# Talking-heads attention before a feed-forward block: values' products of a pair of heads in two halves over two turns

## The chip, the cores and the metric

One core of one Trainium2 chip runs the whole program. The metric is the device time of one execution in microseconds (us), taken over several runs; the profile is of one further execution. The engines are TensorE (PE; its weight loads are shown as PEld), VectorE (DVE), ScalarE (ACT), GpSimd (POOL) and SyncE (SP), whose queue issues most of the DMAs.

## The reference

Four batches, 12 heads, 448 tokens, 64 values a head. The heads are mixed twice: the scores before the softmax (w_pre) and the weights after it (w_post).

```python
scores = scale * np.matmul(q, k.transpose(0, 1, 3, 2))
scores = np.einsum('bhij,hg->bgij', scores, w_pre)
scores = scores - np.max(scores, axis=-1, keepdims=True)
attn = np.exp(scores)
attn = attn / (np.sum(attn, axis=-1, keepdims=True) + 1e-09)
attn = np.einsum('bhij,hg->bgij', attn, w_post)
out = np.matmul(attn, v)             # then (tokens, 768) = x
g = x @ w_gate
silu = g * (1.0 / (1.0 + np.exp(-g)))
y = silu * (x @ w_val) @ w_out
```

## The kernel before, in words

The attention works in **turns**. A turn belongs to one **unit** of 20 tokens of one batch (two tiles of 10 tokens); there are 23 units in a batch, the last of 8 tokens. Each engine runs its instructions in the order in which they are issued, and that order is written out by hand: `at(key, fn)` puts a step at a key, the steps are sorted by key, and a turn is two keys long (`slot(u)` is the key at which the turn of unit u begins; batch b begins at key 45 b, so the short turn 22 is only one key ahead of turn 0 of the next batch). Unit and turn numbers below start with 0 in each batch.

What one turn holds, in the order of its keys:

- `gather` of the unit three turns ahead: 448 KB of scores, which lie in DRAM as rows (token, head), come to SBUF as `rs` (L305). It goes through SP's queue.
- `pre` (key + 0.5, L324): the head mixing w_pre, as 4 products on PE, into two PSUM banks of the tag "pre".
- `qk` (+ 0.55, L275): scores of a group of rows for a unit many turns ahead, into two banks "qk"; VectorE or ScalarE copy them to `stg` (L284, L286), and `store` writes 448 KB to DRAM. Turns 14 to 22 do this for the next batch, turns 0 to 11 for their own; turns 12 and 13 have no scores to make.
- `kprep` (+ 0.65, L228): in turns 10 to 15, the transposes of the keys of one pair of heads of the next batch; `qprep` (+ 0.66, L245): in eight turns of a batch, the transposes of half a block of queries. Both write a bank of the tag "tr", which VectorE empties (`kcopy`, L236, and `qcopy`, L252).
- `top` and `expo` (+ 0.6 and + 0.95): VectorE's row maximum (L335) and ScalarE's exponential (L341) of the two `pre` banks; `norm`: the reciprocal on VectorE and `rw`, w_post divided by the sums, on POOL (L352).
- `post` (L368): 28 small products that mix the exponentials of a unit by `rw`, into the two banks "post"; ScalarE copies them to `attnT` (`mixed`, L383). Its key is that of its own unit + 5.2, which is two turns later, + 1.2: behind `pre`, `qk` and the transposes of that turn.
- `av` (+ 1.3, L410): the products of the mixed weights with the values of one pair of heads, 16 products (32 records) over 240 or 208 tokens, into two banks of the tag "tr" (one for each tile of a unit, r = 0 and 1). Twelve turns of a batch have one: turns 14 to 19 for the first 240 tokens, turns 2 to 7 of the next batch for the rest. `values` (+ 1.9) copies the banks out on ScalarE (L445; L454 and VectorE's L456 for batches 2 and 3).

`attnT` holds 18 units as a ring of three segments; where an `av` wraps round its end, the copies out are in more pieces. The eight PSUM banks are qk 2, pre 2, post 2, tr 2. Batch 3 does its `av` in another pattern at its end, which the change leaves as it is. The feed-forward part follows, and its weights are converted beside the last batch.

Of the kernel before, what the change touches and what calls it, by code (L numbers as in the profile page):

```python
# [24 lines left out]
def talking_heads_moe_kernel(ctx, tc, q, k, v, w_pre, w_post, w_gate, w_val, w_out, out):  # L25
# [25 lines left out]
    NSEG = 3  # L51
# [36 lines left out]
    rsp = pool(right, "rsp", 6, "right")  # L88
    ep = pool(right, "ep", 6, "right")
# [17 lines left out]
    attnT = cst.tile([P, NSEG * SU, NSL, TS], F32, name="attnT")  # L107
    mixing = []

    def mixing_loads():  # L110
        for t, value in ((copies, 0.0), (blocks, 1.0), (wpre, 0.0), (wpost, 0.0)):
            nc.gpsimd.memset(t, value)
        for x, r in itertools.product(range(2), range(2)):
# [38 lines left out]
    qn, kn, vn, kk, qt, stg, rs, pts, sts, et, rw, ats, trs, qtrs, qks = ({} for _ in range(15))  # L152
# [11 lines left out]
    def load_v(b, c):  # L164
        full = S - PART
        if b not in vn:
            vn[b] = vp.tile([P, H, NC, D], F32, tag="vn", name=f"vn_{b}")
        if c < NC:
            hs = slice(c * (H // NC), (c + 1) * (H // NC))
            nc.sync.dma_start(  # L170
                out=vn[b][:, hs, :NC - 1].rearrange("p h c d -> p h (c d)"),
                in_=v[b, hs, :full].rearrange("h (p c) d -> p h (c d)", c=NC - 1),
            )
        else:
            r = c - NC
            nc.sync.dma_start(
                out=vn[b][r * HB:(r + 1) * HB, :, NC - 1], in_=v[b, :, full:].rearrange("h p d -> p h d")
            )
# [6 lines left out]
    def load_k(b, p, part=None, eng=nc.sync):  # L185
# [13 lines left out]
        else:  # L199
# [3 lines left out]
            t = nat.tile([P, n], F32, tag="kn", name=f"kn_{b}_{p}", bufs=6)  # L203
# [34 lines left out]
    def qprep(b, c, g):  # L238
# [3 lines left out]
        tr = ps.tile([P, NPAIR // 2, P], F32, tag="tr", name=f"qtr_{b}_{c}_{g}")  # L242
# [18 lines left out]
    def qk(b, c, g):  # L261
        o, pairs = groups(b, c)[g]
        bank = "qk"
        if b == 0 and c < 2 and (c + g) % 2:
            bank = "pre" if c else "tr"
        pt = [
            ps.tile([P, S], F32, tag=bank, name=f"qk_{b}_{c}_{g}_{x}")
            for x in range(2)
# [10 lines left out]
        stg[b, c, g] = nat.tile([P, 2, S], F32, tag="stg", name=f"stg_{b}_{c}_{g}", bufs=6)  # L279
# [65 lines left out]
    def norm(b, u):  # L345
# [4 lines left out]
        for r, t in enumerate(tiles_of(u)):  # L350
            w = rw[b, t] = smp.tile([P, H, HS], F32, tag="rw", name=f"rw_{b}_{t}", bufs=6)
# [24 lines left out]
    def mixed(b, u, y):  # L376
        pt = ats[b, u][y]
        seg, i = divmod(u, SU)
        i += (b * NC + seg) % NSEG * SU
        m = min(HS, rows(2 * u) - y * HS)  # L380
        full = len(tiles_of(u)) == 2
        for part, n0, n1 in ((P, 0, NSL),) if full else ((P, 0, (NC - 1) * H), (HB, (NC - 1) * H, NC * H)):
            nc.scalar.activation(attnT[:part, i, n0:n1, y * HS:y * HS + m], pt[:part, n0:n1, :m], AF.Copy)  # L383
# [4 lines left out]
    def av(b, c0, m, p):  # L388
        n = -(-cols(c0, m) // TS)
        w = SEG // (3 - m)  # L390
        pt = [ps.tile([P, S], F32, tag="tr", name=f"av_{b}_{c0}_{p}_{r}")[:, :SEG] for r in range(2)]
        first = (b * NC + c0) % NSEG
        wrapped = first + m > NSEG
        ring = attnT.rearrange("p (s u) z i -> p s u z i", s=NSEG)
        u0 = first * SU
        for c in range(NC):
            for x in range(3 - m):
                for r in range(2):
                    k = (n + 1 - r) // 2
                    part = slice(r * HB, (r + 1) * HB) if c == NC - 1 else slice(P)  # L400
                    for j in range(2):
                        h = 2 * (p + x) + j
                        js = slice(j * D, (j + 1) * D)
                        if wrapped:
                            o = pt[r][js].rearrange("p (s u i) -> p s u i", s=2, i=TS)
                            a = ring[part, 0:NSEG:NSEG - 1, :, place(r, c) + h]
                        else:
                            o = pt[r][js, x * SEG // 2:x * SEG // 2 + k * TS].rearrange("p (u i) -> p u i", i=TS)
                            a = attnT[part, u0:u0 + k, place(r, c) + h]
                        nc.tensor.matmul(o, vn[b][part, h, c], a, start=(c == 0 and x == 0), stop=(c == NC - 1 and x == 2 - m))  # L410
        avs[b, c0, p] = pt, c0, m, wrapped

    def spread(av, *to):
        pt, c0, m, wrapped = av
        n = cols(c0, m)
        full, rest = divmod(n, 2 * TS)
        for r in range(2):
            if wrapped:
                v = pt[r].rearrange("p (s u i) -> p s u i", s=2, i=HS)
                for s in range(2):  # L420
                    yield v[:, s], *(
                        d[:, 0].rearrange("p (s u r i) -> p s u r i", s=2, r=2, i=HS)[:, 1 - s, :, r] for d in to
                    )
            else:
                v = pt[r].rearrange("p (x u i) -> p x u i", x=3 - m, i=HS)
                yield v[:, :, :2 * full], *(
                    d[:, :, :2 * full * TS].rearrange("p x (u r i) -> p x u r i", r=2, i=HS)[:, :, :, r] for d in to
                )
        if rest and wrapped:
            v = pt[0].rearrange("p (s u i) -> p s u i", s=2, i=TS)[:, 0, full - SU, :rest]  # L430
            yield v, *(d[:, 0, n - rest:n] for d in to)
        elif rest:
# [651 lines left out]
```

## Time and profile before

| | us |
|---|---|
| median of three runs | 898.02 |
| lowest, highest run | 894.50, 1346.31 |
| the profiled execution's own time | 896.03 |
| its span, first to last instruction | 894.2 |
| PE busy in the span | 855.1 |

The profiled execution lasted 1.8 us longer than its span. The attention takes about the first 400 us of the span, the feed-forward block the rest. A stretch that is called a period below is from the start of `pre` in turn 14 of a batch to the same point of the next batch. Starts in the rows are us from the start of the span.

### The profile page before, as it was taken

The numbers are of one execution on the slowest core, as the hardware profiler recorded it, in microseconds if no ns is written. First come the engines' busy times: TensorE is split into PE (matmuls) and PEld (weight loads), VectorE is DVE, ScalarE is ACT, GpSimd is POOL, SyncE is SP. The second block draws the span as 40 slices with busy tenths as digits, with TensorE's granted clock in tenths as the row PEclk, the third lists the DMA queues.
The fourth block names the chain that finished last, engine by engine and source line by source line (L and its number), as shares of the span: only waits on it lengthen the run. The fifth ranks groups of instructions, "written<-read, shape, count | busy, mean of one in ns | idle before, by whom it ended". The sixth has DMA issues, their size and how long they took to land.

```text
span 894.2 us, 26476 instructions
## 1 busy us (share of the span) xinstructions
PE 855.1 (96%) x10886; PEld 703.9 (79%) x10886; DVE 643.5 (72%) x1159; ACT 458.8 (51%) x1042; POOL 175.9 (20%) x255
## 2 busy tenths in 40 slices
PE   8589999999999997989999999999999999999998
PEld 5255666566656665668999999999999999999998
DVE  3476575657666765567999999678999969775843
ACT  3375677667766767653343333254454455353321
POOL 2011111111111111114555453111101112002020
PEclk9698999999999999999999999999999999999999
DMA  9898998989897869344998886446755579988696
GB/s 213 290 297 266 297 283 282 330 265 296 277 336 234 272 211 315 133 146 151 302 313 252 253 285 174 155 154 209 226 183 179 184 271 324 320 281 194 185 285 157
DMA packets 186033, 218.72 MB, mean 245 GB/s; under 512 B 58136, under 2 KB 153400, under 8 KB 185912
## 3 DMA queue, kind: packets, MB, share of 16 engines
q1 hardware_dynamic: 178856, 205.91, 71.7%
q0 software_dynamic: 3168, 8.26, 5.4%
q10 hardware_dynamic: 3888, 2.86, 1.2%
q8 instruction: 86, 1.41, 0.6%
q14 instruction: 35, 0.29, 0.1%
HBM read 138.15 MB, written 77.47 MB: 241 GB/s over the span
## 4 chain that ended last, share of the span: by engine, by line
PE 80%; DMA 8%; DVE 5%; ACT 3%; issue 2%; SPq 0%; POOL 0%; DVEq 0%; ACTq 0%; POOLq 0%
PE pre L324 8%; PE av L410 8%; PE post L368 7%; PE qk L275 6%; PE p L711 6%; PE p L710 6%; PE p L713 6%; PE q L854 4%; PE q L853 4%; PE q L852 4%; PE upv L766 3%; PE upv L765 3%; PE upv L769 3%; PE upg L769 3%; PE upg L765 3%; PE upg L766 3%
## 5 line engine op out<-in xcount | busy, mean ns | idle before, releaser
L335 DVE TENSOR_REDUCE st<-pre 128x1 f32<-128x448 f32 x180 | 104.4, 620 | 78.0 <-PE pre L324 71.7
L341 ACT ACTIVATE e<-pre,st 128x448 f32<-128x448 f32 x180 | 112.7, 631 | 83.3 <-DVE st L335 75.2
L608 POOL TENSOR_SCALAR mag<-mag 128x768 f32<-128x768 f32 x33 | 99.8, 3024 | 257.0 <-ACT mag L606 227.4
L368 PEld LDWEIGHTS post<-rw,e 60*64 60x64 f32 x5040 | 98.7, 136 | 36.4 <-issue 26.7
L352 POOL TENSOR_SCALAR rw<-w_post_gs,st 128x60 f32<-128x60 f32 x180 | 55.6, 324 | 332.8 <-DVE st L349 270.9
L324 PE MATMUL pre<-rs,w_pre_blocks 64*64 64x448 f32 (+1 forms) x720 | 106.7, 569 | 13.4 <-DMA rs<-s_all 8.5
L368 PE MATMUL post<-rw,e 60*64 60x60 f32 x5040 | 105.7, 223 | 8.5 <-issue 4.5
L383 ACT ACTIVATE attnT<-post 128x420 f32<-128x420 f32 (+1 forms) x192 | 91.2, 542 | 23.0 <-PE post L368 22.5
L275 PE MATMUL qk<-kk,qt 64*64 64x448 f32 x672 | 94.4, 547 | 0.4 <-DVE w_post_gs L148 0.3
L854 PE MATMUL q<-ohi,al 128*128 128x384 f32 x276 | 93.3, 338 | 1.4 <-DVE al L837 1.4
L852 PE MATMUL q<-ohi,ah 128*128 128x384 f32 x276 | 93.0, 337 | 0.6 <-ACT ah L845 0.5
L853 PE MATMUL q<-olo,ah 128*128 128x384 f32 x276 | 92.8, 336 | 0.0
L410 PE MATMUL av<-attnT,vn 128*64 128x120 f32 (+9 forms) x1728 | 88.7, 262 | 3.9 <-issue 2.2
L410 PEld LDWEIGHTS av<-attnT,vn 128*64 128x64 f32 (+1 forms) x1728 | 70.0, 135 | 16.3 <-issue 7.9
L284 DVE COPY stg<-qk 128x448 f32<-128x448 f32 x120 | 71.1, 618 | 8.3 <-PE qk L275 5.0
L845 ACT ACTIVATE ah<-ar 128x768 fp32r<-128x768 f32 x46 | 38.6, 843 | 57.6 <-PE q L853 28.8
L275 PEld LDWEIGHTS qk<-kk,qt 64*64 64x64 f32 x672 | 32.1, 134 | 35.3 <-issue 24.0
L837 DVE TENSOR_TENSOR al<-ar,ah 128x768 fp32r<-128x768 f32 x46 | 43.7, 953 | 15.5 <-ACT ah L845 15.5
L854 PEld LDWEIGHTS q<-ohi,al 128*128 128x128 f32 x276 | 51.8, 188 | 2.7 <-DVE al L837 2.7
L606 ACT ACTIVATE mag<-raw 128x768 f32<-128x768 f32 x36 | 32.8, 911 | 40.8 <-DVE w L620 27.8
L766 PE MATMUL upv<-x,wlo 128*128 128x448 f32 x144 | 52.8, 367 | 0.0
L765 PE MATMUL upg<-x,whi 128*128 128x448 f32 x144 | 52.8, 367 | 0.0
(141 smaller groups left out, 1676.8 us busy)
## 6 DMA issues: line engine op xcount, KB each, us to landing
rs<-s_all SPq DMA_DIRECT2D x88, 448.0 KB, 5.2
s_all<-stg SPq DMA_DIRECT2D x60, 448.0 KB, 5.1
w_d<-w SPq DMA_DIRECT2D x36, 384.0 KB, 4.0
raw<-in_moe_w_gate_dram SPq DMA_DIRECT2D x12, 768.0 KB, 5.3
raw<-in_moe_w_val_dram SPq DMA_DIRECT2D x12, 768.0 KB, 6.6
raw<-in_moe_w_out_dram SPq DMA_DIRECT2D x12, 768.0 KB, 5.8
w<-w_d SPq DMA_DIRECT2D x24, 384.0 KB, 5.8
s_all<-stg SPq DMA_DIRECT2D x39, 224.0 KB, 5.0
```

The lines of the kernel that those rows point to most:

```text
L275: nc.tensor.matmul(pt[x][i * HB:(i + 1) * HB], qt[b, c][hs, p, r:r + HB], kk[b, p][hs], start=True, stop=True)
L324: nc.tensor.matmul(pt[r][x * HB:(x + 1) * HB], wpre[i], xs[i, x], start=True, stop=True)
L335: nc.vector.tensor_reduce(sts[b, u][:, 0, r:r + 1], pts[b, t], axis=AX.X, op=ALU.max, negate=True)
L341: nc.scalar.activation(e, pts.pop((b, t)), AF.Exp, bias=st[:, 0, r:r + 1], scale=1.0, accum_out=st[:, 1, r:r + 1])
L368: nc.tensor.matmul(ats[b, u][y][o * HB:(o + 1) * HB, to, :m], et[b, t][i, c * P + x * HB:c * P + (x + 1) * HB], rw[b, t][i, :, :m], start= ...
L410: nc.tensor.matmul(o, vn[b][part, h, c], a, start=(c == 0 and x == 0), stop=(c == NC - 1 and x == 2 - m))
L608: eng.tensor_scalar(mag, mag, f32_of(0x38000000), f32_of(0x47EFFFFF), op0=ALU.max, op1=ALU.min)
L765: nc.tensor.matmul(pt, hi[:, c], xh[:, c, ts], start=(c == 0), stop=False)
L766: nc.tensor.matmul(pt, lo[:, c], xh[:, c, ts], start=False, stop=False)
L852: nc.tensor.matmul(pt, ahi, bhi, start=f == 0, stop=False)
L853: nc.tensor.matmul(pt, ahi, blo, start=False, stop=False)
L854: nc.tensor.matmul(pt, alo, bhi, start=False, stop=f == NFH - 1)
```

## The change

The ring goes: `attnT` holds all 23 units of a batch (16.8 KB more in each partition), so an `av` never wraps. To pay for it, the buffers of `rs`, `e` and `rw` go from 6 to 4, those of `kn` and `stg` from 6 to 5. In batches 0 to 2 each `av` is cut in two halves in two turns: the half for r = 0 (its three full blocks of keys), then that for r = 1 with the last block of keys for both. The halves lie in turns 13 to 22, 0 and 1 (first 240 tokens) and 2 (both halves of the first pair) to 12 (the rest). The two "tr" banks become one "av" (r = 0) and one "tr" (r = 1, and all transposes). `post` moves one key forward, to the head of its turn, ahead of `pre`. The first block of queries of the next batch is transposed in turns 7 and 9 in place of 11 and 12, and loaded earlier. The values of a batch come in 9 DMAs in place of 6, in three steps at turns 6.5, 9.5 and 13.25 in place of turns 8 to 12.

```diff
-    rsp = pool(right, "rsp", 6, "right")
-    ep = pool(right, "ep", 6, "right")
+    rsp = pool(right, "rsp", 4, "right")
+    ep = pool(right, "ep", 4, "right")
...
-    attnT = cst.tile([P, NSEG * SU, NSL, TS], F32, name="attnT")
+    attnT = cst.tile([P, NUB, NSL, TS], F32, name="attnT")
...
-            t = nat.tile([P, n], F32, tag="kn", name=f"kn_{b}_{p}", bufs=6)
+            t = nat.tile([P, n], F32, tag="kn", name=f"kn_{b}_{p}", bufs=5)
...
-            tr = ps.tile([P, S], F32, tag="tr", bufs=2, name=f"ktr_{b}_{p}")
+            tr = ps.tile([P, S], F32, tag="tr", bufs=1, name=f"ktr_{b}_{p}")
...
-        tr = ps.tile([P, NPAIR // 2, P], F32, tag="tr", name=f"qtr_{b}_{c}_{g}")
+        tr = ps.tile([P, NPAIR // 2, P], F32, tag="tr" if b or g == 0 else "av", bufs=1, name=f"qtr_{b}_{c}_{g}")
...
-        stg[b, c, g] = nat.tile([P, 2, S], F32, tag="stg", name=f"stg_{b}_{c}_{g}", bufs=6)
+        stg[b, c, g] = nat.tile([P, 2, S], F32, tag="stg", name=f"stg_{b}_{c}_{g}", bufs=5)
...
-    def av(b, c0, m, p):
+    def av(b, c0, m, p, steps=(0, 1)):
         n = -(-cols(c0, m) // TS)
-        pt = [ps.tile([P, S], F32, tag="tr", name=f"av_{b}_{c0}_{p}_{r}")[:, :SEG] for r in range(2)]
...
+        for r in steps:
+            avs[b, c0, p, r] = ps.tile([P, S], F32, tag=("av", "tr")[r], bufs=1, name=f"av_{b}_{c0}_{p}_{r}")[:, :SEG]
+        u0 = c0 * SU
+        for c in range(NC if 1 in steps else NC - 1):
             for x in range(3 - m):
-                for r in range(2):
+                for r in steps if c < NC - 1 else range(2):
...
-        for i, c in enumerate((NC, NC + 1, *range(NC))):
-            at(n0 + 16.2 + 1.6 * i if b else (-34.3, -34.29, -30.35, -30.34, -29.35, -29.34)[i], later(load_v, b, c))
+        if b:
+            for g, n in enumerate((13.0, 19.0, 26.5)):
+                at(n0 + n, later(load_v, b, g))
+                for r in range(2):
+                    at(n0 + n + 0.7 + 0.7 * r, later(load_v_last, b, r, g))
...
-            ready = (slot(BACK - NUB - 3), slot(BACK - NUB - 2)) if c == 0 else (at_k[0] - 2, at_k[2])
+            ready = (slot(BACK - NUB - 7), slot(BACK - NUB - 5)) if c == 0 else (at_k[0] - 2, at_k[2])
...
-            n1 = n + (5.2 if b < B - 1 or u < NUB - 3 else 4.2 if u == NUB - 3 else 3.2)
+            n1 = n + (4.2 if u < NUB - 2 else 3.2)
...
+            if b < B - 1:
+                for p in range(NPAIR):
+                    for i in range(2):
+                        u = 13 + 2 * p + i if c0 == 0 else NUB + 2 if p == 0 else NUB + 1 + 2 * p + i
+                        n = slot(u) if u < NUB else n0 + NTB + 2 * (u - NUB)
+                        at(n + 1.3, later(av, b, c0, m, p, (i,)))
+                    at(n + 1.9, later(values, b, c0, m, p))
+                continue
```

## Rows read from the trace of the kernel before

**Rows 1.** The page, busy time of the span: engine, us, share, instructions.
```profile
PE 855.1 (96%) x10886; PEld 703.9 (79%) x10886; DVE 643.5 (72%) x1159; ACT 458.8 (51%) x1042; POOL 175.9 (20%) x255
```

**Rows 2.** Windows of two periods: stretch, length, busy by engine, clock, DMA share, GB/s.
```profile
82.68:171.30 88.62, 86.98 (x2053) 58.68 (x2045) 56.74 (x140) 63.05 (x193) 13.59 (x45) 1.00 0.91 286
259.62:349.00 89.38, 84.23 (x2019) 56.29 (x2019) 58.97 (x170) 60.51 (x189) 13.59 (x45) 1.00 0.82 262
```

**Rows 3.** Windows of the period between, by turns 14-15, 16-19, 20-1, 2-7, 8-13.
```profile
171.30:182.02 10.72, 10.34 (x216) 6.83 (x220) 5.45 (x13) 6.03 (x17) 1.81 (x6) 1.00 1.02 320
182.02:199.69 17.67, 17.67 (x431) 12.40 (x427) 9.34 (x23) 12.07 (x35) 2.44 (x8) 1.00 0.86 252
199.69:213.71 14.02, 13.48 (x339) 9.48 (x332) 10.68 (x25) 10.52 (x29) 2.12 (x7) 1.00 0.87 275
213.71:239.85 26.14, 26.14 (x631) 17.59 (x634) 15.40 (x39) 18.02 (x60) 3.78 (x13) 1.00 0.87 288
239.85:259.62 19.77, 18.73 (x449) 11.79 (x442) 15.12 (x37) 14.91 (x42) 3.46 (x13) 1.00 1.09 336
```

**Rows 4.** Timeline of PE, turn 18 of batch 1: start, length, line, operation [idle].
```profile
190.91 0.93 PE L324 MATMUL pre<-rs,w_pre_blocks 64*64 64x448 f32 x8
191.66 0.94 PE L275 MATMUL qk<-kk,qt 64*64 64x448 f32 x8
192.42 1.00 PE L368 MATMUL post<-rw,e 60*64 60x60 f32 x56
193.34 1.82 PE L410 MATMUL av<-attnT,vn 128*64 128x120 f32 x32
194.98 0.56 PE L324 MATMUL pre<-rs,w_pre_blocks 64*64 64x448 f32 x4
```

**Rows 5.** Timeline of PE, products over 208 tokens, turn 6 of batch 2.
```profile
234.50 1.64 PE L410 MATMUL av<-attnT,vn 128*64 128x110 f32 x32
235.96 0.92 PE L324 MATMUL pre<-rs,w_pre_blocks 60*64 60x448 f32 x8
```

**Rows 6.** Timeline, turn 15 of batch 1: key transposes, two score copies on VectorE.
```profile
176.75 0.93 PE L324 MATMUL pre<-rs,w_pre_blocks 64*64 64x448 f32 x8
...
179.05 1.04 PE L368 MATMUL post<-rw,e 60*64 60x60 f32 x56
...
179.92 0.61 DVE L236 COPY kk<-ktr 128x448 f32<-128x448 f32 x1
...
180.59 0.51 PEld L410 LDWEIGHTS av<-attnT,vn 128*64 128x64 f32 x10 [0.37 <-DVE kk L236]
```

**Rows 7.** Timeline, turn 16 of batch 1: query transposes, one score copy on VectorE.
```profile
182.02 0.94 PE L324 MATMUL pre<-rs,w_pre_blocks 64*64 64x448 f32 x8
...
184.12 1.16 PE L368 MATMUL post<-rw,e 60*64 60x60 f32 x56
...
184.66 0.55 DVE L252 COPY qt<-qtr 128x384 f32<-128x384 f32 x1
```

**Rows 8.** Timeline, turn 14 of batch 1: key transposes, one score copy on VectorE.
```profile
171.30 0.98 PE L324 MATMUL pre<-rs,w_pre_blocks 64*64 64x448 f32 x8 [0.95 <-ACT attnT L383]
...
173.45 0.61 DVE L284 COPY stg<-qk 128x448 f32<-128x448 f32 x1
...
173.65 0.34 PE L368 MATMUL post<-rw,e 60*64 60x60 f32 x7
...
173.98 0.61 DVE L236 COPY kk<-ktr 128x448 f32<-128x448 f32 x1
```

**Rows 9.** Timeline of SP's queue, turns 13 to 15 of batch 1.
```profile
168.82 3.47 SPq L170 DMA_DIRECT2D vn<-in_v_dram  x1
173.86 1.20 SPq L305 DMA_DIRECT2D rs<-s_all  x2
...
177.87 0.75 SPq L305 DMA_DIRECT2D rs<-s_all  x1
```

**Rows 10.** The page, DMA issues: tile, count, KB each, median us to landing.
```profile
rs<-s_all SPq DMA_DIRECT2D x88, 448.0 KB, 5.2
```

**Rows 11.** Timeline, turn 10 of batch 0: first key transposes.
```profile
67.95 0.90 PE L228 MATMUL ktr<-ident,kn 128*128 128x128 f32 x3 [3.48 <-DMA kn<-in_k_dram]
```

**Rows 12.** Timeline of ACT at the start: the last copy of scores before turn 0.
```profile
24.84 0.54 ACT L286 ACTIVATE stg<-qk 128x448 f32<-128x448 f32 x1 [2.00 <-DMA s_all<-stg]
```

More of the change, by code (lines that the diff above doesn't have):

```diff
@@ L112, in mixing_loads @@
             nc.gpsimd.memset(t, value)
+        nc.gpsimd.memset(attnT[:, NUB - 1, :, S % TS:], 0.0)
         for x, r in itertools.product(range(2), range(2)):
@@ L150, in mixing_blocks @@
             )
-    qn, kn, vn, kk, qt, stg, rs, pts, sts, et, rw, ats, trs, qtrs, qks = ({} for _ in range(15))
+    qn, kn, kk, qt, stg, rs, pts, sts, et, rw, ats, trs, qtrs, qks = ({} for _ in range(14))
     def keys(c):
@@ L162, in row, with load_v, load_v_last @@
         return PART + (c - 1) * P if c else 0
-    def load_v(b, c):
+    vn = vp.tile([P, H, NC, D], F32, name="vn")
+    def load_v(b, g):
         full = S - PART
[L166 to L178, printed above, removed]
+        hs = slice(g * (H // 3), (g + 1) * (H // 3))
+        nc.sync.dma_start(
+            out=vn[:, hs, :NC - 1].rearrange("p h c d -> p h (c d)"),
+            in_=v[b, hs, :full].rearrange("h (p c) d -> p h (c d)", c=NC - 1),
+        )
+    def load_v_last(b, r, g=None):
+        hs = slice(H) if g is None else slice(g * (H // 3), (g + 1) * (H // 3))
+        nc.sync.dma_start(
+            out=vn[r * HB:(r + 1) * HB, hs, NC - 1], in_=v[b, hs, S - PART:].rearrange("h p d -> p h d")
+        )
     def load_q(b, c, eng=nc.sync):
@@ L262, in qk @@
         o, pairs = groups(b, c)[g]
-        bank = "qk"
+        banks = (("qk", 2),) * 2
         if b == 0 and c < 2 and (c + g) % 2:
-            bank = "pre" if c else "tr"
+            banks = (("pre", 2),) * 2 if c else (("tr", 1), ("av", 1))
         pt = [
-            ps.tile([P, S], F32, tag=bank, name=f"qk_{b}_{c}_{g}_{x}")
-            for x in range(2)
+            ps.tile([P, S], F32, tag=tag, bufs=bufs, name=f"qk_{b}_{c}_{g}_{x}")
+            for x, (tag, bufs) in enumerate(banks)
         ]
@@ L402, in av, with spread @@
                         h = 2 * (p + x) + j
[L403 to L414, printed above, removed]
+                        y = x * SEG // 2
+                        o = avs[b, c0, p, r][j * D:(j + 1) * D, y:y + k * TS].rearrange("p (u i) -> p u i", i=TS)
+                        a = attnT[part, u0:u0 + k, place(r, c) + h]
+                        nc.tensor.matmul(o, vn[part, h, c], a, start=(c == 0 and x == 0), stop=(c == NC - 1 and x == 2 - m))
+    def spread(b, c0, m, p, *to):
         n = cols(c0, m)
@@ L417, in spread @@
         for r in range(2):
[L418 to L432, printed above, removed]
-            v = pt[0].rearrange("p (x u i) -> p x u i", x=3 - m, i=TS)[:, :, full, :rest]
-            yield v, *(d[:, :, n - rest:n] for d in to)
+            pt = avs[b, c0, p, r]
+            v = pt.rearrange("p (x u i) -> p x u i", x=3 - m, i=HS)
+            yield v[:, :, :2 * full], *(
+                d[:, :, :2 * full * TS].rearrange("p x (u r i) -> p x u r i", r=2, i=HS)[:, :, :, r] for d in to
+            )
+            if rest and r == 0:
+                v = pt.rearrange("p (x u i) -> p x u i", x=3 - m, i=TS)[:, :, full, :rest]
+                yield v, *(d[:, :, n - rest:n] for d in to)
     def values(b, c0, m, p):
-        av = avs.pop((b, c0, p))
         n = cols(c0, m)
@@ L443, in values @@
             t = xtp.tile([P, 1, 2 * SEG], F32, tag="x", name=f"x_{nm}_{c0}_{c}")
-            for v, h in spread(av, t):
+            for v, h in spread(b, c0, m, p, t):
                 nc.scalar.activation(h, v, AF.Copy, scale=-1.0 if nm[0] == "n" else 1.0)
@@ L544, in talking_heads_moe_kernel @@
                 u = first + p // (3 - m)
-                if u < NUB:
-                    n = slot(u)
-                elif b < B - 1:
-                    n = n0 + NTB + 2 * (u - NUB)
-                else:
-                    n = n0 + NTB + 2.0 + 0.3 * p
+                n = slot(u) if u < NUB else n0 + NTB + 2.0 + 0.3 * p
                 at(n + 1.3, later(av, b, c0, m, p))
-                at(n + (1.9 if u < NUB or b < B - 1 else 1.6), later(values, b, c0, m, p))
+                at(n + (1.9 if u < NUB else 1.6), later(values, b, c0, m, p))
     LEAD = 0.9
     pl = {}
-    banks = itertools.cycle([("qk", 2)] * 2 + [("pre", 2)] * 2 + [("post", 2)] * 2 + [("tr", 2)] * 2)
+    banks = itertools.cycle([("qk", 2)] * 2 + [("pre", 2)] * 2 + [("post", 2)] * 2 + [("tr", 1), ("av", 1)])
     def bank(name):
```

22 lines of the change are left out of this document (9 added, 13 removed).

## The prediction

> **What bounds the kernel now.** I read the page's busy times first: PE is busy 855.1 of 894.2 us [rows 1]. That is no proof that PE has nothing to gain, since an in-order PE that waits between overlapping products still shows as busy. So I read the windows of the attention next. Between turn 14 of one batch and turn 14 of the next lie 88.62, 88.32 and 89.38 us [rows 2, 3] (the middle one is the sum of the five rows of rows 3), at full clock. To see what PE must spend there, I priced one turn's steps from start to start in the timeline: `pre` 0.75 us, `qk` 0.76, `post` 0.92, `av` 1.64 over 240 tokens [rows 4] and 1.46 over 208 [rows 5]. Key transposes add 0.84 us: in turn 14 `post` starts 2.35 us after `pre` where it starts 1.51 after it without them [rows 4, 8]. Query transposes add 0.6 by the same reckoning [rows 4, 7], 0.64 with the short delay behind them; the two half-size ones, some 0.3 each.
>
> A period then needs: 22.5 units x (0.75 + 0.92) = 37.6; 21 `qk` x 0.76 = 16.0; `av` 6 x 1.64 + 6 x 1.46 = 18.6; keys 6 x 0.84 = 5.0; queries 6 x 0.64 + 2 x 0.3 = 4.4. Together 81.6 us. PE thus waits 7.0 us in the first period and 6.7 in the second. The third lacks four key and two small query steps (no batch follows), needs 77.6 and waits 11.8. In all **25.5 us of waits** in the stretch that the change rearranges. That is the whole pot.
>
> Where they lie: in rows 3, turns 16 to 19 need 4 x 4.07 + 2 x 0.64 = 17.6 us and take 17.67; with products in the turn, PE is full. Turns 20 to 1, without products, need about 12.0 (4.5 units, five `qk`, one query step) and take 14.02. Turns 8 to 13 need 17.6 and take 19.77, turns 2 to 7 need 24.6 and take 26.14, turns 14 and 15 need 9.8 and take 10.72 [rows 3]. A turn of bare `pre`, `qk` and `post` (2.43 us) is shorter than the way from `pre` through maximum and exponential back to the free bank; a turn with a product hides that way.
>
> **The change part by part.**
>
> *Halves.* No product is added. Of 32 records, 12 go to the first half (0.6 us) and 20 to the second (1.0). Nearly every turn then holds 3.0 or 3.4 us of PE work, and the bare turns vanish. ScalarE must keep up: it is busy 63.05 of 88.62 us [rows 2], so it has room, though with little to spare within a turn. The gain is bounded by 0 and 25.5 us. I leave 7 of it standing: 1.5 to 2 us a period for late transfers and instruction supply, which no reordering of PE's work touches, and 3.4 in the third period, whose turns 9 to 13 wait far more than the 2.9 us of products moved into turns 9 to 12. So 18.5 us come back.
>
> *One bank for transposes and second halves, and `post` in front.* This is the costly part. Keys are transposed in turns 10 to 15, queries in 2, 8 and 16 among others; second halves lie in the even turns 4 to 22, in 1 and in 2. In turns 8, 10, 12, 14, 16 and 2 both want the single "tr" bank, and the half must wait until VectorE has emptied it. VectorE is late there, because two maxima and one or two score copies are ahead of that copy. Today there are two such banks, and `post` (0.92 us) lies between the transposes and `av`; still, with two score copies ahead, the weights of `av` wait 0.37 us for the key copy [rows 6]. Afterwards `post` has run already and nothing lies between. Counted from `pre`: with one score copy the key copy ends at 173.98 + 0.61 - 171.30 = 3.29 us, while PE is through with the transposes at 2.35 [rows 8]. With 0.06 us to restart (180.53 to 180.59 [rows 6]) the wait is 1.0 us, in turns 10 and 14. For queries the copy ends at 3.19, PE is ready at 2.10 [rows 7]: 1.15 us, in turns 8 and 16. Turn 12 has no `qk` (PE 0.76 earlier) and no score copy (VectorE 0.61 earlier [rows 4, 8]): 1.15 us. Turn 2 has the first half of its own pair in between, so 0.55 is left. A full batch pays 2 x 1.0 + 2 x 1.15 + 1.15 + 0.55 = 6.0; the three periods 6.0 + 6.0 + 3.85 (turns 14, 16, 2 and 8) = 15.9 us. Queued behind the waiting half are the next `post` and `pre`, with maximum and exponential behind them, so all of it lies on PE's path. In the odd turns first halves have the "av" bank for themselves, so the wait of rows 6 itself goes.
>
> The row shows that VectorE's copy out of the bank already ends behind PE with two banks in rotation [rows 6]. The Trainium skill, "Perfetto Trace Analysis", section Optimizing Tensor Performance, says that independent groups of products should rotate through different PSUM banks so that emptying one overlaps the next. It speaks against this edit: by it, the shared turns overlap nothing and the sum ends 15.9 us above one with rotating banks, as the rows say too.
>
> *Fewer buffers.* `rs`: a gather leaves SP's queue at 177.87, after the start of turn 15 at 176.75, for unit 18 [rows 6, 9]. Unit 14, whose buffer it would now take, was read from 171.30 on [rows 8]. So the queue, not the buffer, sets its start: nothing lost, covered by the stores ahead of it in the queue. Without that cover it would cost what the landing exceeds: 5.2 us [rows 10] against three turns of about 3.2 less 1.1, some 8.5 us. `e` and `rw`: two units deep, and `post` of unit u-2 now runs before the exponential of unit u is written: nothing; uncovered, one `post`, 0.92 us a turn. `kn`: a sixth load waits for the transposes of turn 10 and is needed in turn 15: nothing. `stg`: at the start nine groups go through the ring, and a copy already waits 2.00 us for a store [rows 12]; with five buffers the last waits some 6 us longer, but PE has no scores to mix until the first gather lands. Between 0 and 2 us; I take 0.5.
>
> *Loads.* SP issues three more value DMAs a batch, spread over turns 6.5 to 14. Today the last one held the queue 3.47 us, with two gathers behind it [rows 9]. The moved step passes gathers in SP's queue; I count nothing, with -1 to +1 us a period as bounds, and the gathers' 8.5 us of lead as cover.
>
> *First batch.* In turn 10 PE waits 3.48 us for keys [rows 11]. `post` now runs before that wait, and the query load that stood ahead of the keys in SP's queue is gone: a gain of 0.9 to 3. Against it, turns 7 and 10 of that batch have two transposes in the one bank, 1 us each. I take -0.5.
>
> *Copies out.* Batches 0 and 2 lose two ScalarE pieces in half of their `values`; ScalarE is not the bound [rows 2]: nothing.
>
> **Sum.** 896.0 (this execution: span 894.2 and 1.8 around it) - 18.5 + 15.9 + 0.5 - 0.5 = 893.4. That execution is 2 us below the median of the runs shown, so a median may lie at 895 as well. I say **893**.
>
> **The rivals.**
>
> *The waits for the bank do not bite (877 us).* If VectorE's copies come about 1 us earlier than in rows 7 and 8, or the bank is left sooner, the 15.9 us fall away: 893 - 16 = 877, 2.1% faster. For it: the pot is real, and 18.5 us of it cost nothing to take. Against it: maxima, score copy and transpose copy keep their order on VectorE, and nothing in the change moves them.
>
> The Trainium skill, same page, section Optimization Strategy, says that stretches with different limits may be improved by interleaving them; that would be this 877, and here the full and the bare turns of rows 3 are such stretches.
>
> *Transfers set the turns (909 us, slower).* The five stretches move 252 to 336 GB/s, and turns 8 to 13 have the DMA engines full (1.09) [rows 3]. Where turns 14 to 19 today give 4.07 us for a gather and a store of 448 KB each, the even flow gives 3.2. If gathers land later than the 8.5 us of lead, PE waits for `rs` in place of banks, little of the pot comes back (3 in place of 18.5) and the new bank waits come on top: 896 + 15.9 - 3 = 909, 1.4% slower. It decides from a landing of 8.5 us, against a median of 5.2 [rows 10]. Against it: the total moved stays, and the mean share of a period is 0.82 to 0.94 [rows 2, 3].
>
> *The edit does little of either (897).* Turns 2, 14 and 16 keep their length and start-up loses 1 to 3 us through `stg`.
>
> **How the numbers follow.** Forecast (887 to 900) 0.58; 877 case 0.17; 909 case 0.16; the last one 0.09, inside the forecast's span. A measurement of this kernel tells about 2% from no change. Faster by over 2% (below 878 to 880) takes some two thirds of the second case: 0.11. Slower by over 2% (above 914 to 916): the tail of the third, 0.04. The rest 0.85. The range of eight in ten runs from 876 to 909.
>
> **What would show it.** The periods from turn 14 to 14: I expect about 89, 89 and 85 us. Second halves in turns 8, 10, 12, 14 and 16 should start 3.2 to 3.4 us after `pre`, with about 1 us of PE or PEld waiting for L236 or L252. Turns 20 to 1 should show PE without gaps, about 3.0 to 3.4 us each. If PE waits for `rs` instead, the 909 case is on; if the halves start right behind the transposes, the 877 case. The forecast is wrong if the bare turns stay short of work, or if ScalarE, now given `mixed` ahead of the exponentials, holds back the maxima's turn.

## The result, and the profile after

The changed kernel takes **899.26 us** (median of 20 runs, 894.27 to 903.09); the kernel before, run beside it, 894.52 (20 runs). The ratio is **1.006, 95% interval 1.004 to 1.0079**: slower by 0.6%, some 5 us, where 893 and a small gain were forecast. The ratios here are of the fast runs alone, so they differ a little from those of the medians. The time lies inside the forecast's range of 876 to 909. The profiled execution of the changed kernel took 902.21 us, its span is 900.5, 6.3 above that of before.

The page's busy times of the changed kernel, in the form of [rows 1]:

```profile
PE 850.7 (94%) x10886; PEld 682.8 (76%) x10886; DVE 640.0 (71%) x1147; ACT 459.7 (51%) x1018; POOL 178.3 (20%) x256
```

PE runs the same 10886 instructions. Its busy time fell by 4.4 us while the span grew by 6.3, so this view doesn't tell where the time went. The windows do: the start, three periods from turn 14 to turn 14, and the tail to the feed-forward's first product (columns as in [rows 2]: stretch, length, busy time and instructions of PE, PEld, DVE, ACT and POOL, granted clock, DMA share, GB/s).

```profile
0.00:88.96 88.96, 68.25 (x1119) 39.09 (x1122) 44.46 (x104) 40.70 (x100) 12.99 (x53) 0.87 0.94 255
88.96:181.50 92.54, 85.35 (x2059) 52.45 (x2054) 55.13 (x135) 62.52 (x179) 13.12 (x44) 1.00 0.92 287
181.50:272.31 90.81, 85.47 (x2052) 52.50 (x2048) 55.41 (x137) 62.45 (x179) 13.45 (x45) 1.00 0.92 286
272.31:359.43 87.12, 82.02 (x2020) 49.73 (x2012) 58.09 (x160) 61.55 (x178) 13.46 (x45) 1.00 0.81 254
359.43:399.29 39.86, 35.45 (x971) 25.47 (x961) 26.09 (x68) 27.67 (x76) 6.97 (x19) 0.96 0.54 168
```

Before, turn 14 of batch 0 began at 82.68, and the periods were 88.62, 88.32 and 89.38 [rows 2, 3]. So the start lost 6.28 us, the periods 3.92, 2.49 and -2.26 (together 4.15), the tail gained 4.18 (it was 44.04, shown with the eleventh run), and the feed-forward is as long as it was (501.21 us, 501.16 then). Sum: +6.25, the difference of the spans but for that 0.05. The clock in the three periods is full in both kernels. The forecast was 89, 89 and 85 for the periods.

The 4.15 us of the periods can't be told from the spread between executions. Run eleven below changes the last batch alone; its first period, in the order of before and at full clock, took 90.38 us where it was 88.62:

```profile
77.19:167.57 90.38, 86.77 (x2054) 59.11 (x2045) 56.55 (x140) 63.39 (x193) 14.09 (x47) 1.00 0.91 286
```

So the terms below are read from turns and waits that come back alike in several traces, and not from whole periods.

**The bank waits came as forecast.** Turn 14 of batch 1, PE and VectorE in time order, to be read beside [rows 8]:

```profile
181.50 0.97 PE L324 MATMUL pre<-rs,w_pre_blocks 64*64 64x448 f32 x8
...
183.19 0.55 PE L228 MATMUL ktr<-ident,kn 128*128 128x128 f32 x3
183.64 0.61 DVE L284 COPY stg<-qk 128x448 f32<-128x448 f32 x1
...
184.17 0.61 DVE L236 COPY kk<-ktr 128x448 f32<-128x448 f32 x1
...
184.84 1.21 PE L401 MATMUL av<-attnT,vn 128*64 128x120 f32 x20 [0.89 <-DVE kk L236]
```

PE is through with the transposes at about 183.95; the bank is free when VectorE's copy ends at 184.78; the second half starts 3.34 us after `pre`, as forecast (3.2 to 3.4). The PE waits of the whole span (line, what it waited for, us in total, times, longest):

```profile
PE av L401 <- DVE qt L252: 7.2, 9, 1.0
PE av L401 <- DVE kk L236: 6.8, 7, 1.2
```

Together 14.0 us; the forecast was 15.9. By turn: 0.89 to 0.90 in turns 10 and 14 (forecast 1.0), 1.03 to 1.05 in 8 and 16 (1.15), 1.16 in 12 (1.15), 0.32 in 2 (0.55).

**What was not forecast.** The cleanest place is a pair of turns without transposes and waits, 17 and 18 of batch 1, PE alone:

```profile
195.80 0.97 PE L324 MATMUL pre<-rs,w_pre_blocks 64*64 64x448 f32 x8
196.58 0.97 PE L275 MATMUL qk<-kk,qt 64*64 64x448 f32 x8
197.48 0.85 PE L401 MATMUL av<-attnT,vn 128*64 128x120 f32 x12
198.25 1.04 PE L368 MATMUL post<-rw,e 60*64 60x60 f32 x56
199.12 0.97 PE L324 MATMUL pre<-rs,w_pre_blocks 64*64 64x448 f32 x8
199.90 0.97 PE L275 MATMUL qk<-kk,qt 64*64 64x448 f32 x8
200.80 1.21 PE L401 MATMUL av<-attnT,vn 128*64 128x120 f32 x20
201.84 0.99 PE L368 MATMUL post<-rw,e 60*64 60x60 f32 x56
202.65 0.57 PE L324 MATMUL pre<-rs,w_pre_blocks 64*64 64x448 f32 x4
```

From start to start the odd turn takes 3.32 us and the even one 3.53: 6.85. Before, a turn with a whole pair took 4.07 [rows 4], and a bare one needs 2.43 by the same rows, together 6.50. No wait is recorded in either, and the products are the same 32 records: 0.35 us more. One sees where: from `qk` to `av` it is 0.90 us, to `post` it was 0.76 [rows 4], and the 12 records of the first half take 0.77, not 0.6.

Not all of it is the cut's. In this trace `pre` to `qk` takes 0.78 us throughout, where [rows 4] have 0.75. Run nine below has the same products in its periods; there `pre` to `qk` takes 0.76 and `qk` to `av` 0.86. Its turns 3 and 4 of batch 3, a pair over 208 tokens:

```profile
314.30 0.93 PE L324 MATMUL pre<-rs,w_pre_blocks 60*64 60x448 f32 x8
...
317.49 0.94 PE L324 MATMUL pre<-rs,w_pre_blocks 64*64 64x448 f32 x8
...
320.82 0.93 PE L324 MATMUL pre<-rs,w_pre_blocks 60*64 60x448 f32 x8
```

They take 3.19 and 3.34 us, 6.53, where a whole pair and a bare turn need 3.89 and 2.43 [rows 4, 5], 6.32: 0.21 more. So **a cut pair costs PE 0.21 to 0.35 us where no transposes are near**.

Beside transposes it costs less. Turns 9 and 10 of batch 2 have them both: they begin at 251.97 and 255.56 and end at 260.63, 0.89 us of it a bank wait, which leaves 7.76; the prediction's prices give 2 x 2.43 + 1.46 + 0.60 + 0.84 = 7.76, so the cut costs nothing. Turns 19 and 20 of batch 1 (202.65 to 209.99), with transposes in the first alone, take 7.34 against 7.10: 0.24. A batch has 11 cut pairs, since the first pair of the rest has both halves in turn 2. Of the 33 in three batches 11 are free of transposes, 10 have them in one turn and 12 in both. By these prices they cost some 7 us in this trace and some 3 us by the turns of run nine (0.21, 0.08 and nothing); both are estimates. The 4 us between them lie in `pre` and `qk` and not in the cut; why this trace has them slower stays open.

**The start.** VectorE's last copy of scores ahead of the first maximum, in the kernel before and in the changed one:

```profile
24.23 0.62 DVE L284 COPY stg<-qk 128x448 f32<-128x448 f32 x1 [1.22 <-DMA s_all<-stg]
32.43 1.16 DVE L335 TENSOR_REDUCE st<-pre 128x1 f32<-128x448 f32 x2 [7.57 <-PE pre L324]
```

```profile
34.94 0.62 DVE L284 COPY stg<-qk 128x448 f32<-128x448 f32 x1 [7.82 <-DMA s_all<-stg]
35.48 1.15 DVE L335 TENSOR_REDUCE st<-pre 128x1 f32<-128x448 f32 x2
```

In the changed kernel that copy waits 7.82 us for a store to empty a buffer of the ring; the first maximum is 3.05 us later. In turn 7 PE then waits 3.32 us for gathered scores. SP's queue ahead of that gather:

```profile
47.39 2.15 SPq L183 DMA_DIRECT2D qn<-in_q_dram  x2
49.59 5.27 SPq L294 DMA_DIRECT2D s_all<-stg  x2
54.95 0.54 SPq L305 DMA_DIRECT2D rs<-s_all  x1
```

### The profile page after: what moved, and what is told of

Its sections match the earlier page's. It is cut to its first block, busy times and chain, and to the rows that moved or that the text cites. A ratio compares the mean times of both kernels' runs of the same rounds, so it can differ in the third digit from the quotient of the medians.

```text
span 900.5 us, 26491 instructions
## 1 busy us (share of the span) xinstructions
PE 850.7 (94%) x10886; PEld 682.8 (76%) x10886; DVE 640.0 (71%) x1147; ACT 459.7 (51%) x1018; POOL 178.3 (20%) x256
## 4 chain that ended last, share of the span: by engine, by line
PE 81%; DMA 8%; DVE 7%; issue 2%; ACT 1%; SPq 0%; POOL 0%; ACTq 0%; POOLq 0%; DVEq 0%
PE av L401 9%; PE post L368 9%; PE pre L324 8%; PE p L703 6%; PE p L701 6%; PE p L700 6%; PE qk L275 5%; PE q L844 4%; PE q L842 4%; PE q L843 4%; PE upv L756 3%; PE upv L755 3%; PE upv L759 3%; PE upg L759 3%; PE upg L755 3%; PE upg L756 3%
## 5 line engine op out<-in xcount | busy, mean ns | idle before, releaser
L324 PE MATMUL pre<-rs,w_pre_blocks 64*64 64x448 f32 (+1 forms) x720 | 98.3, 579 | 17.4 <-DMA rs<-s_all 10.6
L401 PE MATMUL av<-attnT,vn 128*64 128x120 f32 (+9 forms) x1728 | 94.4, 263 | 18.2 <-DVE qt L252 7.2
L368 PE MATMUL post<-rw,e 60*64 60x60 f32 x5040 | 98.8, 223 | 3.0 <-issue 2.1
L368 PEld LDWEIGHTS post<-rw,e 60*64 60x64 f32 x5040 | 89.9, 137 | 15.0 <-issue 8.8
L275 PE MATMUL qk<-kk,qt 64*64 64x448 f32 x672 | 87.7, 565 | 0.3 <-DVE w_post_gs L148 0.3
L275 PEld LDWEIGHTS qk<-kk,qt 64*64 64x64 f32 x672 | 28.2, 138 | 39.7 <-issue 28.4
L755 PE MATMUL upv<-x,whi 128*128 128x448 f32 x144 | 52.8, 367 | 0.0
```

The costliest lines, as they stand in the source:

```text
L275: nc.tensor.matmul(pt[x][i * HB:(i + 1) * HB], qt[b, c][hs, p, r:r + HB], kk[b, p][hs], start=True, stop=True)
L324: nc.tensor.matmul(pt[r][x * HB:(x + 1) * HB], wpre[i], xs[i, x], start=True, stop=True)
L368: nc.tensor.matmul(ats[b, u][y][o * HB:(o + 1) * HB, to, :m], et[b, t][i, c * P + x * HB:c * P + (x + 1) * HB], rw[b, t][i, :, :m], start= ...
L401: nc.tensor.matmul(o, vn[part, h, c], a, start=(c == 0 and x == 0), stop=(c == NC - 1 and x == 2 - m))
L755: nc.tensor.matmul(pt, hi[:, c], xh[:, c, ts], start=(c == 0), stop=False)
```

## The experiments

My theory after the result: cutting the products costs PE time by itself; the bank waits are real; the start is lost to smaller buffers or early loads. The expectations of the fifth run and the sixth count 12 cut pairs a batch; there are 11. The ratios are each against the kernel before, run beside it on the same chip.

**The cut by itself.** Run twelve changes nothing else in the kernel before (shown without the new argument of `av`):

```
-  at(n + 1.3, later(av, b, c0, m, p))
+  if b < B - 1 and u in (17, 18, NUB + 3, NUB + 4, NUB + 6, NUB + 7):
+      at(n + 0.52, later(av, b, c0, m, p, (0,)))
+      at(n + 1.3, later(av, b, c0, m, p, range(1, NC)))
+  else:
+      at(n + 1.3, later(av, b, c0, m, p))
```

> The kernel before with the value products of a pair cut in two within one turn: the first quarter goes between pre and qk, the rest stays behind post; only in turns without transposes (17, 18, 3, 4, 6 and 7; 6 a batch, 18 in all). No product is added, no bank and no buffer changes, no turn gives work to another. Theory (each time PE goes to the value products and back costs 0.24 to 0.35 us): a clean turn takes 4.3 to 4.4 us in place of 4.07, 4.3 to 6.3 us in all, ratio 1.005 to 1.007. Rival (the cost in the changed kernel lay in its banks, or in the second half's start): the clean turns stay at 4.07, ratio 1.000.

Measured: 897.4 us, ratio **1.004 (1.0014 to 1.0066)**. A turn of it, PE alone:

```profile
187.48 0.93 PE L324 MATMUL pre<-rs,w_pre_blocks 64*64 64x448 f32 x8
188.35 0.63 PE L412 MATMUL av<-attnT,vn 128*64 128x120 f32 x8
188.91 0.98 PE L275 MATMUL qk<-kk,qt 64*64 64x448 f32 x8
189.71 0.99 PE L368 MATMUL post<-rw,e 60*64 60x60 f32 x56
190.63 1.41 PE L412 MATMUL av<-attnT,vn 128*64 128x120 f32 x24
191.86 0.56 PE L324 MATMUL pre<-rs,w_pre_blocks 64*64 64x448 f32 x4
```

4.38 us against 4.07, with no wait in the turn: +0.31 for one more visit to the value products, whose 8 and 24 records take 0.56 and 1.23 in place of 1.64 together, and which start 0.87 after `pre` where `qk` starts 0.75 after it. Of the twelve cut turns in the periods of batches 0 and 1, eleven are 0.30 to 0.31 us longer than the same turns need whole. 18 x 0.31 = 5.6 us lies inside the interval (1.3 to 5.9 us). In batch 2 the earlier quarter also waits for VectorE's copies out of its bank, 1.3 us in five visits, so the whole time alone does not price the cut; the turns do. The cost of an extra visit is shown, without any change of bank, buffer or turn.

Run five takes the cut out of the changed kernel:

```
-  u = 13 + 2 * p + i if c0 == 0 else NUB + 2 if p == 0 else NUB + 1 + 2 * p + i
+  u = 14 + 2 * p if c0 == 0 else NUB + 2 + 2 * p
```

> The changed kernel with the two halves of each pair's products in the same (even) turn; every other line stays. Theory (each cut of a pair costs PE 0.35 us for changing from qk's products to av's and back, 12 pairs a batch, and the first half ahead of the second would cover most of a bank wait): 4.2 us a batch less for the cuts and some 3.4 of the 5.4 us of bank waits less, against some 4.8 us of waits in odd turns that are bare again (0.4 each): periods of about 88 us, 891 in all. Rival (the cut costs nothing, the time lies in the waits): periods some 1.4 us longer than the changed kernel's, 903. Two turns with a pair together should last 6.5 us where no transposes are, in place of 6.85.

Measured: 895.34 us, ratio 1.0002 (0.9975 to 1.0029), an interval below that of the changed kernel; the rival's 903 is out. Its bank waits are down from 14.0 to 2.7 us, since the first half now covers most of each:

```profile
PE av L401 <- DVE qt L252: 1.9, 6, 0.4
...
PE av L401 <- DVE kk L236: 0.8, 2, 0.4
```

With 11.3 us of waits gone, and the 7 us of cuts and slower `pre` and `qk` (0.76 and 0.86 here too), one would expect some 18 us less in the periods. They are 90.01, 89.59 and 87.17, only 3.7 less in all: the 33 turns of the first halves have no products again and give back the rest, 0.44 us for each (expected 0.4). Turns 17 and 18 of batch 1 show it, from 193.80 over 196.34 to 201.06: 2.54 and 4.72 us, 7.26 together where 6.50 are needed, with no wait of over 0.04 recorded. So cutting does cure bare turns: the cut pair takes 6.85, and 0.21 above need by run nine, so 0.41 to 0.55 of these 0.76 us come back. What the cure gives is about what the bank waits take.

Run six cuts the changed kernel's first half once more:

```
+  if i == 0 and p and not (c0 == 0 and p == 5):
+      at(n + 0.52, later(av, b, c0, m, p, (i,), (0,)))
+      at(n + 1.3, later(av, b, c0, m, p, (i,), range(1, NC)))
...
```

> The changed kernel with the first half cut once more in 9 of 12 pairs a batch: its first third goes between pre and qk, so PE changes to the value products and back two times in place of one in an odd turn. No product is added. Theory (changing costs): 0.25 to 0.35 us more for each of 27 cuts, 7 to 9.5 us more than the changed kernel (899 to 907), and the clean odd turn 3.32 -> 3.6 to 3.7 us. Rival (the 0.35 us of a cut pair is latency of the second half or of its bank, not the changing): 0, odd turns stay at 3.3.

Measured: 903.88 us, ratio 1.0087 (1.0056 to 1.0119); the interval overlaps that of the changed kernel, so the time alone doesn't decide. The clean odd turn does:

```profile
200.38 0.94 PE L324 MATMUL pre<-rs,w_pre_blocks 64*64 64x448 f32 x8
201.25 0.43 PE L401 MATMUL av<-attnT,vn 128*64 128x120 f32 x4
201.60 0.98 PE L275 MATMUL qk<-kk,qt 64*64 64x448 f32 x8
202.51 0.63 PE L401 MATMUL av<-attnT,vn 128*64 128x120 f32 x8
203.08 1.04 PE L368 MATMUL post<-rw,e 60*64 60x60 f32 x56
203.94 0.94 PE L324 MATMUL pre<-rs,w_pre_blocks 64*64 64x448 f32 x8
```

3.56 us against 3.32: +0.24, the lower end of what was expected. Against turn 17 of batch 1 in run nine (3.25 us, 188.69 to 191.94), which has `pre` and `qk` as fast as this trace, it is +0.31, as in run twelve. 27 x 0.24 = 6.5 us; the two ratios differ by 2.4 us, uncertain by over 3, so the runs don't confirm the total.

**The bank.** Run three puts `post` in front in the kernel before, which keeps whole products and two banks:

```
-  n1 = n + (5.2 if b < B - 1 or u < NUB - 3 else 4.2 if u == NUB - 3 else 3.2)
+  n1 = n + (4.2 if u < NUB - 2 else 3.2)
```

> The kernel before with the mixing products (post) at the head of their turn as in the changed kernel, nothing else. Theory that post was the cover of the transposes' copies: in turns 2, 5, 14, 15, 16 and 19 the second products of av wait 0.9 to 1.6 us for VectorE's copy in place of 0 to 0.6, some 5 to 6 us more in each of the three periods, and a gain of about 4 us in the last batch (the changed kernel gained 4.2 there): 8 to 14 us longer. Rival (the place of post is free, the bank waits of the changed kernel come from the single bank alone): 0 to 4 us shorter.

Measured: 901.78 us, ratio 1.0092 (1.0056 to 1.0127), with these waits of PE:

```profile
PE av L410 <- DVE qt L252: 9.2, 12, 1.3
...
PE av L410 <- DVE kk L236: 5.0, 6, 1.1
```

14.2 us against 1.2 in the kernel before. `post` between the transposes and `av` was the cover that the prediction took it for; a second bank doesn't help as long as `av` takes both. So much of the wait comes with `post` in front alone; no run has one bank with `post` behind the transposes.

Run four moves the changed kernel's transposes to the stretch between `post` and `pre`, with VectorE's copy ahead of the maxima (the keys are shown; the queries alike, but for the earliest blocks of batch 0):

```
-  at(n + 0.65, later(kprep, b, p))
-  at(n + 0.8, later(kcopy, b, p))
+  at(n + 0.4, later(kprep, b, p))
+  at(n + 0.45, later(kcopy, b, p))
```

> The changed kernel with the transposes of keys and queries moved from behind qk to between post and pre, and VectorE's copy of them ahead of the maxima. Theory (one bank for transposes and second halves costs what was forecast): the waits of av for L236 and L252 (5.4 us in a full batch) vanish, the three periods from turn 14 to 14 fall from 92.5, 90.8 and 87.1 to about 87, 85.5 and 84 us, the run by 12 to 16 us to about 885, faster than the kernel before. Rival (the wait moves: the transposes now wait for ScalarE's copy of the half before them, or VectorE starts the maxima late): 0 to 4 us gained.

Measured: 901.47 us, ratio 1.0082 (1.0054 to 1.011): no gain. The waits of `av` for VectorE's key and query copies are gone from the list; the transposes now wait for the bank instead, until the copies of the mixed values (`x`) have emptied it:

```profile
PE av L401 <- DVE x L435: 2.1, 3, 1.7
...
PE ktr L228 <- ACT x_b L424: 1.5, 3, 0.8
PE ktr L228 <- ACT x_n L424: 1.5, 3, 0.8
...
PE qtr L245 <- ACT x_n L424: 1.4, 3, 0.5
```

With 2.2 us more in smaller rows the transposes wait 6.6 us, and `av` another 2.1 for VectorE's part of those copies. One bank for two users makes one of them late, whichever goes first; and the transposes, taken from beside `av`, add changes between kinds of products (argued, from the prices above).

**Buffers, loads and the start.** Run one has the score ring of five alone, in the kernel before (`stg` with `bufs=5`):

> The kernel before with one buffer less for the staged scores (stg 5 in place of 6), nothing else. Theory: this is half of the 6.3 us that the changed kernel is late at turn 14 of batch 0 (88.96 in place of 82.68). The last score copy before turn 0 should wait for a store until about 35 us in place of 24.8, the first maximum start at about 35.5 in place of 32.4, turn 14 at about 85.7; the whole run 2 to 4 us longer. Rival (the lateness comes from the gather buffers or the queue alone): 0 to 1 us.

Measured: 897.69 us, ratio 1.0044 (1.0015 to 1.0072). Its start:

```profile
32.68 0.62 DVE L284 COPY stg<-qk 128x448 f32<-128x448 f32 x1 [7.50 <-DMA s_all<-stg]
33.23 1.14 DVE L335 TENSOR_REDUCE st<-pre 128x1 f32<-128x448 f32 x2
```

The last copy comes 8.45 us later than before (24.23), the first maximum only 0.80. Turn 0 is 1.9 us longer, yet turn 14 begins at 81.03, earlier than before. The trace doesn't show the 4 us that the runs lost.

Run two loads the next batch's first query block early in the kernel before (`slot(BACK - NUB - 7)` and `- 5` for `- 3` and `- 2`):

> The kernel before with the first block of queries of the next batch loaded and transposed as early as in the changed kernel (turns 7 and 9 of the batch before, load four turns ahead), nothing else. Theory: two query loads then stand together in SP's queue in turn 3 of batch 0, the gathers behind them land late, PE waits about 3 us for one of them near turn 8 and its clock falls; turn 14 of batch 0 comes 2 to 4 us later and the run is 2 to 4 us longer. Rival (the wait for a gather in the changed kernel comes from four gather buffers in place of six): no change here, within 1 us.

Measured: 895.78 us, ratio 1.0005 (0.9975 to 1.0035): nothing.

Run seven has four gather buffers in the kernel before (`rsp` 4 for 6):

> The kernel before with four buffers for gathered scores in place of six, nothing else. Theory (at the start, and there alone, the gathers wait for buffers and SP's queue stands behind them): turns 0 to 13 of batch 0 some 3 to 6 us longer than the 52.05 of before, waits of pre for rs near turn 7 as in the changed kernel (3.3 us), later periods within 1 us: 896 to 899. Rival (what is late at the start is the queries, loaded early, or the score ring): 0, 893.5.

Measured: 893.22 us, ratio 0.9976 (0.9945 to 1.0007): nothing, and turns 0 to 13 of batch 0 take 51.16 us. My theory fell.

Run eight has `post` in front, as run three, and all the smaller buffers (`rsp`, `ep` and `rw` 4, `kn` and `stg` 5):

> The kernel before with post in front and all the smaller buffers of the change (scores gathered 4, exponentials 4, weights 4, keys 5, score ring 5), products whole and loads as before. Theory (buffers cost at the start only): the 901.8 us of the kernel with post in front alone, plus 4 to 7 at the start: 906 to 909; turns 0 to 13 of batch 0 take 55 us or more in place of 49.2. Rival (buffers cost nothing once post is in front, the start is lost to the loads): 901 to 903.

Measured: 904.26 us, ratio 1.0085 (1.0054 to 1.0117), beside the 1.0092 of run three: the time lies between theory and rival, and the ratios show no loss from buffers that the runs can tell. The profiled start is longer, 54.43 us for turns 0 to 13 against 49.16, most of it in turn 10, which takes 8.97 us, 3.37 of them a wait for keys of the kind that [rows 11] show, where run three's takes 5.16.

Run nine is the changed kernel with the query block two turns later in batch 0 (`ready[0] - 4` for `- 8` there):

> The changed kernel with the next batch's first query block loaded two turns later in batch 0 only (SP's queue then has one query load, not two, ahead of the stores and the gather for turn 7). Theory (the early query load pushes that gather late at the start): the 3.3 us wait of turn 7 for its scores is gone or below 1 us, turns 0 to 13 of batch 0 some 3 us shorter (58.7 to 55 or 56), 896. Rival (four gather buffers do it): the wait stays, 899.

Measured: 897.07 us, ratio 1.0039 (1.0009 to 1.0068). Turns 0 to 13 of batch 0 take 51.72 us in place of 58.73, and the wait for scores in turn 7 is down from 3.32 to 0.56, as the theory had it. But in the same turn PE now waits for the query block itself:

```profile
59.79 0.37 PE L245 MATMUL qtr<-ident,qn 64*128 64x64 f32 x3 [2.57 <-DMA qn<-in_q_dram]
```

The interval overlaps that of the changed kernel; whether the 7 us of the trace hold in the runs is not settled (the two ratios differ by 2 us, uncertain by over 3).

**A better kernel.** Run ten joins run five, run nine and `post` of the first unit one turn later in batch 0 (`5.2 if b == u == 0`):

> The changed kernel with both halves of a pair in one turn, the query block two turns later in batch 0, and post of the first unit of batch 0 one turn later, behind pre of turn 2. Theory (each mends its own loss: 0.35 us a cut pair, 3 us at turn 7, 1.5 us at turn 1): 895.3 - 3 - 1.5 = 891, turns 0 to 13 of batch 0 below 55 us, below the kernel before by 0.3 to 0.5%. Rival (what the start gives back is lost to the next transfer): 895.

Measured: 895.2 us, ratio 1.0034 (1.0 to 1.0068). It does not beat the kernel before. It differs from run nine by whole products and the late `post`, and its ratio is the same within some 4 us; so the 5 us between run five and the changed kernel did not come a second time. The late `post` met a wait of its own, and the start came out at 86.33:

```profile
PE post L368 <- POOL rw L352: 2.4, 1, 2.4
```

Run eleven puts `post` in front in the last batch alone, in the kernel before:

```
-  n1 = n + (5.2 if b < B - 1 or u < NUB - 3 else 4.2 if u == NUB - 3 else 3.2)
+  n1 = n + (5.2 if b < B - 1 or u < 11 else 4.2 if u < NUB - 2 else 3.2)
```

> The kernel before with post in front of pre in the last batch alone, from turn 13 on (no key transposes there, so no bank to wait for). Theory (post in front is what shortens the tail of the changed kernel by 4 us): the stretch from turn 14 of the last batch to the feed-forward falls from 44.0 to 38 to 40 us, 4 us in all, 889.5. Rival (the tail varies by itself, 39.8 to 43.5 in kernels that don't touch it; post in front does nothing): within 1 us of before, 893 to 895.

Measured: **891.8 us, ratio 0.9971 (0.9945 to 0.9998)**, the one kernel whose interval lies below 1, by little (0.2 to 4.9 us). The tail, first of the kernel before, then of this one:

```profile
349.00:393.04 44.04, 37.65 (x1013) 28.25 (x1013) 26.13 (x68) 28.87 (x79) 5.84 (x19) 0.96 0.46 154
```

```profile
349.10:385.34 36.24, 32.96 (x969) 24.29 (x965) 25.84 (x68) 27.49 (x76) 6.97 (x19) 0.99 0.49 169
```

7.8 us in the traces, 2.6 in the runs. Part of the difference is the tail's own spread: in four kernels that leave it alone (runs one, two, seven and twelve) it took 43.54, 39.83, 41.37 and 42.67. With `post` in front it was 36.2 to 39.9 in all nine traces.

## Why the prediction failed

Two steps failed. The first is **"Halves. No product is added"**, and with it the price of 0.6 and 1.0 us for the two parts: the 1.64 us of [rows 4] were divided by records, as if a visit to these products cost nothing in itself. A cut pair costs 0.21 to 0.35 us, and an extra visit within a turn 0.31 in run twelve and 0.24 to 0.31 in run six. For 33 pairs that is some 3 to 7 us that the sum doesn't have. The trace of before has no such cut, and `post` always stood between `qk` and `av`; so the price was an unknown and should have been bounded from both sides, not set to nothing.

The second is **"First batch"**, with the ring of five: taken as -0.5 and +0.5, nothing together. In the profiled execution the start lost 6.28 us, most of it in waits: for a store, for the first exponentials behind it, and for scores.

The forecast gain of 2.6 us was the difference of two large terms, 18.5 and 15.9, which each came out within 2 us. So the terms that were set to nothing decided its sign.

What PE does in an extra visit: `pre`, `qk` and `post` run as 64*64 or 60*64 products side by side, `av` as 128*64 over all rows. The Trainium skill, "TensorEngine Tiling (Array Packing)", section Tiling Modes, says that changing the tiling mode, not merely the tile, drains TensorE. By this rule a cut adds two drains where no transposes are near. Count the changes between the three kinds (products over 64 rows, `av`, transposes) over both turns of a pair, before and after the cut: without transposes they go from 2 to 4, with transposes in one turn from 4 to 5, with transposes in both they stay at 6. The costs are 0.35, 0.24 and 0 to 0.13 us in the changed kernel's trace, and 0.21, 0.08 and nothing in run nine's. So the price follows the number of changes and not that of visits, which is one more in each. That agrees with the rule, but no run separates a drain from other costs of a change, so the mechanism stays argued. Only the price is shown.

The other steps, one by one:

- **The pot.** The periods need 81.6, 81.6 and 77.6 us by the prediction's reckoning; they take 92.54, 90.81 and 87.12, 29.7 more. 14.0 of that are the bank waits and some 7 the cuts with the slower `pre` and `qk`, which leaves 8.7 of other waits, where 25.5 stood before and 7 were to be left. So some 16.8 us came back (by balance), near the forecast 18.5: the bare turns did vanish, at a price. Two of the other waits are recorded: 1.82 us before `pre` in turn 5 of batch 1, and 1.33 in turn 0 of batch 3, where a first half waits for VectorE to empty the "av" bank that it was to have for itself. The pot was also 1.1 us too large: in the first period of before, where the six over 208 tokens wrap round the ring, they take 1.64 us each and not 1.46 (turns 3, 6 and 7 of batch 1 last 4.07 us).
- **One bank, `post` in front.** Right in place and size: 14.0 us for 15.9. The rule of the Trainium skill that was weighed there ("Perfetto Trace Analysis", section Optimizing Tensor Performance: independent groups should rotate through PSUM banks) agrees with the waits of 0.89 to 1.16 us. But run three, with two banks and `post` in front, waits 14.2 us: the place of `post` makes as long a wait as one bank with it, and a second bank that the same `av` takes is no rotation. The 877 case is out.
- **Buffers.** `rs` at nothing: right (run seven). The ring of five was mis-sized at 0.5: alone it cost 4 us (1.3 to 6.4) in run one, while run eight, with `post` in front, shows no cost of all the buffers together. Why the one and not the other stays open.
- **First batch.** Turns 0 to 13 take 56.2 to 61.5 us in the changed kernel and in runs four, five, six and ten, and 48.2 to 52.1 in the kernel before and in runs one, two, seven, eleven and twelve, so this loss is no accident of one trace. The early query load ahead of the gather for turn 7 made the 3.32 us wait there; moved by two turns (run nine), it took that wait away and made another, and the start came to 51.72 (run ten, with the same move and the wait of its late `post`, has 56.54). Early queries alone cost nothing in the kernel before (run two), so it takes them together with something else of the change, and what that is stays open. `post` in front of the wait for keys saved nothing that can be told apart. The 909 case had the right kind of wait there, though only there.
- **The tail** was left out of the sum. `post` in front shortens it, 4.18 us in the trace, and run eleven shows the gain by itself (2.6 us in the runs).

The sum with these sizes, for the profiled execution: 896.0 - 16.8 + 14.0 + 7.0 + 6.3 - 4.2 = 902.3, against 902.21 measured. It closes because the 16.8 is a balance, so it proves nothing. Without the 7.0 or without the 6.3 it would stand at 895 or 896, no change; without both at 889, a small gain, as forecast.

## What to carry to other kernels

Before you cut a group of products to fill short turns, price the cut and not only the products: look for a place in the trace where PE goes from the one kind to the other and compare start to start. Count how often PE changes between products of 64 and of 128 rows in a turn; here one more visit, at 0.21 to 0.35 us, cost a quarter to a half of the idle time that it filled (0.76 us for a bare turn and the one behind it), and nothing where transposes stood beside it in both turns. When a forecast is the difference of two large terms, bound the small ones before you trust its sign. And look for the part of a change that works without the rest: `post` in front lost 0.9% in the whole kernel, where transposes share their banks with `av`, and won 0.3% (0.02 to 0.55%) in the last batch, where no key is transposed.

## What the runs showed of the hardware that was not expected

A visit of PE to products over 128 rows between products over 64 rows costs 0.24 to 0.31 us beyond its records, at full clock and without a recorded wait: 4.07 to 4.38 us for the same 32 records and neighbours (run twelve), 3.32 or 3.25 to 3.56 (run six). About 0.11 to 0.14 of it stands ahead of the visit (`pre` to `av` 0.87 where `pre` to `qk` is 0.75; `qk` to `av` 0.86 to 0.90 where `qk` to `post` is 0.76), most of the rest in the visit. Beside transposes a cut that adds no change between kinds costs nothing (7.76 us for turns 9 and 10, as priced). PE shows as busy throughout, so the page's busy time counts such a cost as work.
